# A decode block on one core: the wait ahead of the unit loop, and a full-width last chunk in the MLP

## The chip, the cores and the metric

One core of a Trainium2 chip runs the kernel. The metric is device time in microseconds (us) of one execution. Engines: TensorE (PE, with its weight loads as PEld), VectorE (DVE), ScalarE (ACT), GpSimd (POOL) and SyncE (SP), which issues nearly all DMA transfers from one in-order queue.

## The reference

Four tokens, each with its own cache of 4096 positions and 32 heads of 128. The caches are bf16 and fill nearly all of the 283 MB that are read.

```python
B, Sq, D, H, Sk, Dh, F = 4, 1, 640, 32, 4096, 128, 1728
q = (layernorm(x) @ wq)                      # per head, B x H x 1 x Dh
p = softmax(einsum("bhqd,bhkd->bhqk", q, k_cache) * Dh ** -0.5)
o = einsum("bhqk,bhkd->bhqd", p, v_cache)
h = x + o @ wo
f = layernorm(h) @ w1 + b1
sp = log1p(exp(-abs(f))) + where(f > 0, f, 0)
h2 = h + (f * tanh(sp)) @ w2                 # B x 1 x D, bf16
```

## The kernel before

**Units and slots.** The attention is cut into 16 units (`NU`), one token and eight heads each. A unit reads one K tile and one V tile of 128 partitions x 64 KiB (8.39 MB each). Three slots of that size in SBUF (`NS`) take them in turn: K of unit u goes into slot 2u mod 3 (unit 0: slot 1), and V of the same unit later into the same slot, once K is used up. Each slot has one DMA semaphore, `slot0` to `slot2`, that both loads count up. "K2" and "V2" stand for the loads of unit 2 below.

**A unit's work.** `scores` multiplies K by the broadcast query in eight steps on DVE (`times_q`, L585, in place), sums over the head dimension on PE through an identity (`sums`, L597), and reduces what is left on DVE (L572). `softmax` finds the maxima and takes the exponentials on ACT (L682). `pv` multiplies the probabilities of the unit before by its V (L707). `close` normalises the unit two before.

**Order.** The outer loop over u emits, for each unit: `scores(u)` (with pieces of `close(u-2)` and the query of u+1 in between), the load of V(u), `pv(u-1)`, the load of K(u+2), `softmax(u)`. So SP issues V(u) when PE has finished the sums of unit u, whose K lies in that slot, and K(u+2) when `pv(u-1)` is done with its slot.

**The planner.** A class `Program` collects the operations with what they read and write, and sets the semaphore waits. An operation has a key whose last entry is the unit in which it is emitted; a DMA has a semaphore of its own name in `sem`. All engines but PE run straight code. PE's work of units 2 to 13 is a hardware loop of 4 turns over 3 units (`Fori`, L200), whose waits count with the turn. Ahead of the loop PE waits for everything in `pe_entry` (L127 to 136, L198): for each source the latest operation that some PE step of the loop needs and that has no key or a key below unit 2. V1 is such an operation: it is loaded in unit 1 and read in unit 2 by `pv(1)`. `pv`'s own wait on the slot's semaphore is in the loop's body as well (`body_waits`).

**The end.** When K15 and V14 are used, their slots take the weights of the rest: SP issues four loads of wo, five of w1 (`load`, L823), the last 64 rows of w2 (`w2r_sb`), and w2's 13 full blocks of 128 rows in four loads. `load` waits for the last readers of the bytes that it overwrites; for w2 that is `last_pv`, which is `pv(14)`. Then `regroup` and `project` multiply by wo, `column_means` and three DVE steps make the second layernorm, `h1_pass` (L956) does the 14 column chunks of w1 for each of five row blocks, DVE and ACT make the activation `act_t` (a reciprocal and an exponential), and `w2_products` (L1024) sums the 14 chunks, the odd one first. F = 1728 is 13 x 128 + 64: `C2` = 13 full chunks, `FM` = 1664, `FREM` = 64, `FC` = 14 chunks in all. `f_chunk` gives the columns of a chunk; the last has 64, so the upper half of its partitions is set to zero in PSUM by DVE (L950) and in b1T by POOL (L389).

Of the kernel before, what the change touches and what calls it, by code (L numbers as in the profile page):

```python
# [21 lines left out]
class Program:  # L22
# [53 lines left out]
    def plan(self):  # L76
        by_key = {o.key: o for o in self.ops if o.key is not None}

        def shifted(o, units):
            return by_key.get((*o.key[:-1], o.key[-1] + units)) if o.key else None  # L80


        known = {e: {} for e in self.ENGINES}
        for o in self.ops:
            k = known[o.eng]
            o.waits = []
            for src, d in o.deps.items():
                if k.get(src, -1) < d.nth:
                    k[src] = d.nth
                    o.waits.append(d)  # L90


        span = self.last - self.first + 1
        assert span % self.turn == 0
        turns = span // self.turn
        self.turns = turns
        ref0 = self.first + 2 * self.turn
        body = [o for o in self.ops if self.in_loop(o) and ref0 <= o.key[-1] < ref0 + self.turn]
        self.body = body
        before, rest = [], None  # L100
        in_order = [o for o in self.ops if o.eng == "PE"]
        at = [i for i, o in enumerate(in_order) if self.in_loop(o)]
        assert at == list(range(at[0], at[0] + len(body) * turns))
        for t in range(turns):
            for p, b in enumerate(body):
                o = in_order[at[0] + t * len(body) + p]
                assert o is shifted(b, (t - 2) * self.turn), (o.key, b.key)
        self.pe_before = in_order[: at[0]]
        self.pe_after = in_order[at[0] + len(body) * turns :]
        body_waits = [[d for d in b.waits] for b in body]  # L110
        for b in body:
            for d in b.waits:
                assert d.key is not None and d.key[-1] >= self.first + self.turn, (b.key, d.key)


        loop_units = range(self.first, self.last + 1)
        for o in self.ops:
            for d in o.waits:
                d.signal = True
        for o in self.ops:  # L120
            if o.signal and o.key and o.key[-1] in loop_units:
                for u in range(self.first, self.last + 1):
                    same = by_key.get((*o.key[:-1], u))
                    if same is not None and same.sem is None:
                        same.signal = True

        self.pe_entry = {}  # L127
        first_pe = in_order[at[0]].nth
        for p in range(at[0], at[0] + len(body) * turns):
            for src, d in in_order[p].deps.items():  # L130
                if d.key is None or d.key[-1] < self.first:
                    e = self.pe_entry.get(src)
                    if e is None or e.nth < d.nth:
                        self.pe_entry[src] = d
        for d in self.pe_entry.values():
            d.signal = True

        counts = {}
        for o in self.ops:
            src = o.sem or o.eng  # L140
            if o.sem:
                counts[src] = counts.get(src, 0) + 16
            elif o.signal:
                counts[src] = counts.get(src, 0) + 1
            o.count = counts.get(src, 0)
        self.totals = counts


        self.body_waits = []
        for b, waits in zip(body, body_waits):  # L150
            out = []
            for d in waits:
                src = d.sem or d.eng
                e = shifted(d, self.turn)
                step = e.count - d.count
                assert step > 0
                for t in range(turns):
                    f = shifted(d, (t - 2) * self.turn)
                    if f is not None and f.key[-1] >= self.first:
                        assert f.count == d.count + (t - 2) * step, (b.key, d.key, t)  # L160
                base = d.count - 2 * step
                assert base > 0, (b.key, d.key)
                out.append((src, base, step))
            self.body_waits.append(out)


        level = {s: d.count for s, d in self.pe_entry.items()}
        for t in range(turns):
            for p, b in enumerate(body):
                for src, base, step in self.body_waits[p]:  # L170
                    level[src] = max(level.get(src, 0), base + t * step)
                o = in_order[at[0] + t * len(body) + p]
                for src, d in o.deps.items():
                    assert level.get(src, 0) >= d.count, (o.key, d.key, t)
# [35 lines left out]
def kernel(  # L210
# [13 lines left out]
    nc = tc.nc  # L224

    B, Sq, D = A_x.shape
    _, H, Sk, Dh = A_k_cache.shape
    F = B_w1.shape[1]
# [25 lines left out]
    FREM = F - FM  # L254
    FC = C2 + 1
    W2P = (0, 6, 10, 12, C2)


    pad = -int(nc.sbuf_base) % 512
# [126 lines left out]
        w=["ident_f"],  # L386
    )
    P.add("POOL", lambda: nc.gpsimd.memset(ones_f[:, :], 1.0), w=["ones_f"])
    P.add("POOL", lambda: nc.gpsimd.memset(b1T[:, :], 0.0), w=["b1T"])  # L389
    P.add("POOL", lambda: nc.gpsimd.memset(mean_f[:, :], 1.0 / D), w=["mean_f"])  # L390
    P.add("DVE", lambda: nc.vector.memset(eps_t[:, :], EPS), w=["eps"])
    P.add("DVE", lambda: nc.vector.memset(nscale[:, :], -SCALE), w=["nscale"])
# [93 lines left out]
        "DVE", lambda: nc.vector.tensor_copy(out=j_m[:, :], in_=j_f[:, :]), r=["j_f"], w=["j_m"]  # L486
    )

    def f_chunk(rows, c):
        if c < C2:  # L490
            return rows[:, c * 128 : (c + 1) * 128], 128
        return rows[:, FM:F], FREM


    qT_ps = qq_bank[:, 0 : N * H].rearrange("p (b h) -> p b h", b=N)

# [15 lines left out]

    def b1_turned():
        for c in range(FC):
            cols, fw = f_chunk(b1_row, c)
            ins = nc.tensor.matmul(  # L516
                b_ps[0:fw, c : c + 1], lhsT=cols, rhs=ident[0:1, 0:1], start=True, stop=True
            )
        return ins

    def b1_copy():
        nc.vector.tensor_copy(out=b1T[:, 0:C2], in_=b_ps[:, 0:C2])  # L522
        return nc.vector.tensor_copy(out=b1T[0:FREM, C2:FC], in_=b_ps[0:FREM, C2:FC])

    P.add("PE", b1_turned, r=["b1", "ident"], w=[OT])
    P.add("DVE", b1_copy, r=[OT], w=["b1T"])

    def q_broadcast(u, now):
        o, b = divmod(u, N)
# [279 lines left out]
    w1_view = B_w1.rearrange("(c p) n -> p c n", p=128)  # L809
    nw2 = FC * D  # L810
    w2_sb = wend2[:, 0 : C2 * D].rearrange("p (k n) -> p k n", k=C2)
    w2r_sb = wend2[0:FREM, C2 * D : nw2]
    w2_view = B_w2[0:FM, :].rearrange("(k p) n -> p k n", k=C2)

    def load(out_ap, in_ap, i, lo, hi, name):

        ops = {}
        for cell in cells(i, lo, hi):
            for d in P.readers.get(cell, {}).values():
                ops[d.nth] = d  # L820
        P.add(
            "SP",
            lambda: nc.sync.dma_start(out=out_ap, in_=in_ap),  # L823
            w=[name],
            sem="_".join(map(str, name)),
            after=ops.values(),
        )
# [2 lines left out]
        load(wo_sb[:, o], wo_view[:, o], i1, o * J * D, (o + 1) * J * D, ("wo", o))  # L830
    for c in range(DC):
        load(w1_sb[:, c], w1_view[:, c], i1, nwo + c * F, nwo + (c + 1) * F, ("w1", c))
    load(w2r_sb, B_w2[FM:F, :], i2, C2 * D, nw2, ("w2", C2))
    for k0, k1 in zip(W2P, W2P[1:]):
        load(w2_sb[:, k0:k1], w2_view[:, k0:k1], i2, k0 * D, k1 * D, ("w2", k0))

# [110 lines left out]
    tt(sq, hc, hc, ALU.mult, ["hc"], ["sq"])  # L947

    h1_ps = qq_bank[:, 0 : FC * N].rearrange("p (c n) -> p c n", c=FC)
    do("DVE", lambda: nc.vector.memset(h1_ps[FREM:128, FC - 1, :], 0.0), (), [QQ])  # L950
    std, rstd = scratch(N), scratch(N)

    def h1_pass(dc):
        for c in (0, C2, *range(1, C2)):
            lhsT, fw = f_chunk(w1_sb[:, dc, :], c)
            ins = nc.tensor.matmul(  # L956
                h1_ps[0:fw, c, :],
                lhsT=lhsT,
                rhs=h2T[:, dc, :],
                start=(dc == 0 and c == 0),  # L960
                stop=(dc == DC - 1 and c == C2 - 1),
            )
        return ins

# [53 lines left out]

    def w2_products(blocks):
        for c in blocks:  # L1020
            rows = 128 if c < C2 else FREM
            w2 = w2_sb[:, c, :] if c < C2 else w2r_sb
            for dc in range(DC):
                ins = nc.tensor.matmul(  # L1024
                    y2T[:, dc, :],
                    lhsT=w2[:, dc * 128 : (dc + 1) * 128],
                    rhs=act_t[0:rows, c, :],
                    start=(c == C2 and dc == 0),
                    stop=(c == C2 - 1 and dc == DC - 1),
                )  # L1030
        return ins

    for name, blocks in ((C2, [C2]), *((k0, range(k0, k1)) for k0, k1 in zip(W2P, W2P[1:]))):
        do("PE", lambda blocks=blocks: w2_products(blocks), [("w2", name), "act"], [S_BANK[1]])
    oT = scratch(N * DC, BF16).rearrange("p (n c) -> p n c", n=N)
    tt(oT.rearrange("p n c -> p c n"), hT, y2T, ALU.add, ["hT", S_BANK[1]], ["oT"])
    o_ps = tr_bank[0 : N * DC, 0:128]
# [45 lines left out]
```

## Time and profile before

| | |
|---|---|
| median of 3 runs | 672.83 us (672.2 to 672.95) |
| profiled execution | 673.69 us; its span, first to last instruction, 671.8 us; mean granted TensorE clock 0.818 |
| busy | PE 380.5 us (57%), DVE 353.2 (53%), ACT 88.0 (13%), POOL 1.3 |
| SP's DMA queue | 283.35 MB, busy 98.2% of 16 engines' span, mean 422 GB/s |
| chain that ended last | DMA 39%, DVE 28%, PE 20%, another queue or core 8%, SP's queue 3% |

Lines of the profile name the source line (L597), the engine, the operation, the tile written and the tiles read. A row of a timeline or a chain starts with its start and its length in us. In a table by stage each engine's busy time stands in the order PE, PEld, DVE, ACT, POOL, with the number of instructions in brackets, and then PE's granted clock, the DMA engines' busy share and GB/s. The releaser of a wait is inferred from semaphore events.

### The profile page before, as it was taken

To read this page: it belongs to the slowest core of one execution; us is meant where nothing else is said; L and a number is where in the kernel's file an instruction comes from. 1 tells how busy PE (TensorE), PEld (TensorE's weight loads), DVE (VectorE), ACT (ScalarE), POOL (GpSimd) and SP (SyncE) were. 2 spreads that over 40 slices of the span, in tenths; PEclk is the share of its full clock that TensorE was granted. 3 is DMA by queue.
4 is the path that set the end of the run, shared out by engine and by line. 5 is a ranking of instruction groups with operands and counts; after the bars stand their busy time and mean duration, and the time that the engine had idled before them with its cause. 6 is when DMAs were issued, how large, how long until landed. Compare 5 with 4: busy or idle time off the path is not lost.

```text
span 671.8 us, 6600 instructions
## 1 busy us (share of the span) xinstructions
PE 380.5 (57%) x2793; PEld 174.8 (26%) x2793; DVE 353.2 (53%) x314; ACT 88.0 (13%) x314; POOL 1.3 (0%) x10
## 2 busy tenths in 40 slices
PE   0366732887282856738184664818375481837764
PEld 0222310333031322213032321303132230313344
DVE  2078840766381836548182754728184563819501
ACT  0102020020202020110202020020202002020211
POOL 0000000000000000000000000000000000000000
PEclk9999975989596796959688796968879695978965
DMA  9999999799999999999999999999999999999997
GB/s 375 438 437 434 433 435 433 328 376 438 433 434 437 437 437 437 433 437 433 421 425 419 437 437 437 433 437 433 433 437 433 437 437 437 434 430 410 412 416 245
DMA packets 8347, 283.62 MB, mean 422 GB/s; under 512 B 835, under 2 KB 2567, under 8 KB 3208
## 3 DMA queue, kind: packets, MB, share of 16 engines
q1 hardware_dynamic: 8318, 283.35, 98.2%
q8 instruction: 12, 0.20, 0.1%
q14 instruction: 7, 0.06, 0.0%
q10 hardware_dynamic: 10, 0.01, 0.0%
HBM read 283.35 MB, written 0.01 MB: 422 GB/s over the span
## 4 chain that ended last, share of the span: by engine, by line
DMA 39%; DVE 28%; PE 20%; another core or an unknown queue 8%; SPq 3%; issue 1%
DMA slot<-in_A_k_cache_dram 33%; DVE slot L585 23%; PE bank L597 14%; PE bank L707 5%; DMA slot<-in_A_v_cache_dram 4%; DVE s_sb L572 3%; SPq L823 3%; DMA slot<-in_B_w_dram 2%; PE bank L665 0%; DVE mx L652 0%; PE bank L643 0%; DVE otn L767 0%; DVE rl L760 0%; PE bank L741 0%
## 5 line engine op out<-in xcount | busy, mean ns | idle before, releaser
L597 PE MATMUL bank<-slot,ident 128*128 128x512 bf16 x1024 | 273.9, 423 | 250.2 <-DVE slot L585 225.6
L585 DVE TENSOR_TENSOR slot<-slot,qb 128x4096 bf16<-128x4096 bf16 x128 | 288.2, 2284 | 145.4 <-DMA slot<-in_A_k_cache_dram 145.4
L597 PEld LDWEIGHTS bank<-slot,ident 128*128 128x128 bf16 x1024 | 101.5, 107 | 408.4 <-DVE slot L585 258.7
L572 DVE TENSOR_REDUCE s_sb<-bank 128x64 f32<-128x512 f32 x64 | 44.0, 688 | 74.5 <-PE bank L597 74.5
L682 ACT ACTIVATE e<-s_sb,nb 128x256 bf16<-128x256 f32 x128 | 63.1, 494 | 46.6 <-DVE nb L674 46.6
L707 PE MATMUL bank<-slot,e 128*32 128x512 bf16 x1024 | 60.7, 391 | 1.5 <-DMA slot<-in_A_v_cache_dram 1.5
L552 ACT CAST qb<-bank 128x128 bf16<-128x128 f32 x16 | 4.2, 265 | 294.5 <-PE bank L543 294.5
L727 ACT COPY o_sb<-bank 128x512 f32<-128x512 f32 x16 | 9.4, 585 | 200.2 <-PE bank L707 200.2
L707 PEld LDWEIGHTS bank<-slot,e 128*32 128x32 bf16 x1024 | 26.5, 99 | 34.1 <-issue 9.0
L652 DVE TENSOR_REDUCE mx<-bank 1x8 f32<-1x128 f32 x16 | 4.5, 279 | 39.9 <-PE bank L643 39.9
L682 ACT ACTIVATION_READ_ACCUMULATOR e<-s_sb,nb 128x1 f32 x128 | 23.9, 187 | 0.0
L741 PE MATMUL bank<-sel,o_sb 128*128 128x8 f32 x128 | 17.4, 263 | 0.0
L741 PEld LDWEIGHTS bank<-sel,o_sb 128*128 128x128 f32 x128 | 16.4, 201 | 0.0
L500 PE MATMUL bank<-xT,slot 128*128 128x4 bf16 x160 | 4.4, 168 | 11.0 <-DMA slot<-in_A_wq_dram 11.0
L665 PE MATMUL bank<-mx,nscale 1*128 1x8 f32 x32 | 6.1, 262 | 5.9 <-DVE mx L652 5.9
L760 DVE RECIPROCAL rl<-bank 128x8 f32<-128x8 f32 x16 | 3.2, 202 | 11.3 <-PE bank L741 11.3
L522 DVE COPY b1T<-bank 128x13 f32<-128x13 f32 x1 | 0.2, 172 | 14.5 <-PE bank L516 14.5
L665 PEld LDWEIGHTS bank<-mx,nscale 1*128 1x128 f32 x32 | 4.7, 183 | 10.6 <-DVE mx L652 10.6
L500 PEld LDWEIGHTS bank<-xT,slot 128*128 128x128 bf16 x160 | 4.3, 104 | 11.1 <-DMA slot<-in_A_wq_dram 11.1
L634 DVE TENSOR_REDUCE pm<-s_sb 128x1 f32<-128x256 f32 x16 | 6.7, 420 | 0.5
L739 PEld LDWEIGHTS bank<-rs,ones_f 128*128 128x128 f32 x32 | 6.1, 198 | 3.2 <-ACT o_sb L727 1.2
L643 PE MATMUL bank<-ident_f,pm 128*1 128x128 f32 x32 | 6.1, 272 | 1.2 <-DVE pm L634 1.2
(73 smaller groups left out, 69.2 us busy)
## 6 DMA issues: line engine op xcount, KB each, us to landing
slot<-in_A_v_cache_dram SPq DMA_DIRECT2D x4, 2048.0 KB, 42.5
slot<-in_A_wq_dram SPq DMA_DIRECT2D x1, 5120.0 KB, 15.5
slot<-in_A_wo_dram SPq DMA_DIRECT2D x4, 1280.0 KB, 33.8
slot<-in_B_w_dram SPq DMA_DIRECT2D x5, 432.0 KB, 29.7
slot<-in_B_w_dram SPq DMA_DIRECT2D x1, 960.0 KB, 20.4
slot<-in_B_w_dram SPq DMA_DIRECT2D x1, 640.0 KB, 19.5
slot<-in_B_w_dram SPq DMA_DIRECT2D x1, 320.0 KB, 10.9
slot<-in_A_k_cache_dram SPq DMA_DIRECT2D x16, 50.2
```

The source lines that it names most:

```text
L500: ins = nc.tensor.matmul(qT_ps[:, :, h], lhsT=wq_sb[:, c, h * Dh : (h + 1) * Dh], rhs=xT[:, c, :], start=(c == 0), stop=(c == DC - 1),)
L572: lambda: nc.vector.tensor_reduce(out=s_sb[:, part * RP : (part + 1) * RP], in_=s_bank[part][:, :].rearrange("p (r w) -> p r w", w=W), axi ...
L585: return nc.vector.tensor_tensor(out=kt, in0=kt, in1=qbs[u % NS][:, k * DQ : (k + 1) * DQ] .unsqueeze(1) .to_broadcast([128, RP, DQ]), op= ...
L597: ins = nc.tensor.matmul(s_bank[part][:, :].rearrange("p (r w) -> p r w", w=W), lhsT=ident[:, :], rhs=kt[:, :, d : d + W], start=(d == 0), ...
L634: lambda: nc.vector.tensor_reduce(out=pm[:, :], in_=s_sb[:, :], axis=AX.X, op=ALU.max),
L643: lambda: nc.tensor.matmul(tr_bank[0:1, 0:128], lhsT=pm[:, :], rhs=ident_f[:, :], start=True, stop=True),
L665: lambda: nc.tensor.matmul(nb_ps, lhsT=nscale[:, :], rhs=mx[:, :], start=True, stop=True),
L682: ins = nc.scalar.activation(out=e2[:, :, h, :], in_=s_sb[:, :].rearrange("p (g r) -> p g r", r=RQ), func=ACT.Exp, bias=nb[:, h : h + 1], ...
L707: ins = nc.tensor.matmul(o_bank[t : t + G * RQ, :], lhsT=e2[:, g, :, :], rhs=vt[:, g * RQ : (g + 1) * RQ, :], start=(g < CT), stop=(g >= N ...
L727: lambda: nc.scalar.copy(out=o_sb[:, :], in_=o_bank[:, :]),
L741: ins = nc.tensor.matmul(o_ps, lhsT=o_sb[:, r * Dh : (r + 1) * Dh], rhs=sel[:, r, :], start=(r == 0), stop=(r == RQ - 1),)
L823: lambda: nc.sync.dma_start(out=out_ap, in_=in_ap),
```

## The change

1. `pe_entry` takes only operations that are not transfers: an operation with a `sem` is left out. PE no longer waits for transfers ahead of the loop; the waits in the loop's body stay.
2. The last chunk of h1 covers the last 128 columns of w1 and b1 (1600 to 1727), so 64 columns are computed twice. `f_chunk`, POOL's memset of b1T and DVE's memset in PSUM go, the two copies of b1T become one, and the chunks are done in plain order.
3. w2's last 64 rows go to partitions 64 to 127 of `w2r_sb`; partitions 0 to 63 hold zeros, written over the whole tile by a new POOL memset that waits for `last_pv`. The load follows that memset, and PE's product of this chunk uses all 128 rows.

```diff
@@ -128,7 +128,8 @@
         first_pe = in_order[at[0]].nth
         for p in range(at[0], at[0] + len(body) * turns):
             for src, d in in_order[p].deps.items():
-                if d.key is None or d.key[-1] < self.first:
+
+                if d.sem is None and (d.key is None or d.key[-1] < self.first):
                     e = self.pe_entry.get(src)
                     if e is None or e.nth < d.nth:
                         self.pe_entry[src] = d
@@ -254,6 +255,7 @@
     FREM = F - FM
     FC = C2 + 1
     W2P = (0, 6, 10, 12, C2)
+    OVER = 128 - FREM
 
 
     pad = -int(nc.sbuf_base) % 512
@@ -386,7 +388,6 @@
         w=["ident_f"],
     )
     P.add("POOL", lambda: nc.gpsimd.memset(ones_f[:, :], 1.0), w=["ones_f"])
-    P.add("POOL", lambda: nc.gpsimd.memset(b1T[:, :], 0.0), w=["b1T"])
     P.add("POOL", lambda: nc.gpsimd.memset(mean_f[:, :], 1.0 / D), w=["mean_f"])
     P.add("DVE", lambda: nc.vector.memset(eps_t[:, :], EPS), w=["eps"])
     P.add("DVE", lambda: nc.vector.memset(nscale[:, :], -SCALE), w=["nscale"])
@@ -486,11 +487,6 @@
         "DVE", lambda: nc.vector.tensor_copy(out=j_m[:, :], in_=j_f[:, :]), r=["j_f"], w=["j_m"]
     )
 
-    def f_chunk(rows, c):
-        if c < C2:
-            return rows[:, c * 128 : (c + 1) * 128], 128
-        return rows[:, FM:F], FREM
-
 
     qT_ps = qq_bank[:, 0 : N * H].rearrange("p (b h) -> p b h", b=N)
 
@@ -512,18 +508,18 @@
 
     def b1_turned():
         for c in range(FC):
-            cols, fw = f_chunk(b1_row, c)
+            f0 = c * 128 if c < C2 else F - 128
             ins = nc.tensor.matmul(
-                b_ps[0:fw, c : c + 1], lhsT=cols, rhs=ident[0:1, 0:1], start=True, stop=True
+                b_ps[:, c : c + 1],
+                lhsT=b1_row[:, f0 : f0 + 128],
+                rhs=ident[0:1, 0:1],
+                start=True,
+                stop=True,
             )
         return ins
 
-    def b1_copy():
-        nc.vector.tensor_copy(out=b1T[:, 0:C2], in_=b_ps[:, 0:C2])
-        return nc.vector.tensor_copy(out=b1T[0:FREM, C2:FC], in_=b_ps[0:FREM, C2:FC])
-
     P.add("PE", b1_turned, r=["b1", "ident"], w=[OT])
-    P.add("DVE", b1_copy, r=[OT], w=["b1T"])
+    P.add("DVE", lambda: nc.vector.tensor_copy(out=b1T[:, :], in_=b_ps), r=[OT], w=["b1T"])
 
     def q_broadcast(u, now):
         o, b = divmod(u, N)
@@ -809,7 +805,7 @@
     w1_view = B_w1.rearrange("(c p) n -> p c n", p=128)
     nw2 = FC * D
     w2_sb = wend2[:, 0 : C2 * D].rearrange("p (k n) -> p k n", k=C2)
-    w2r_sb = wend2[0:FREM, C2 * D : nw2]
+    w2r_sb = wend2[:, C2 * D : nw2]
     w2_view = B_w2[0:FM, :].rearrange("(k p) n -> p k n", k=C2)
 
     def load(out_ap, in_ap, i, lo, hi, name):
@@ -830,7 +826,18 @@
         load(wo_sb[:, o], wo_view[:, o], i1, o * J * D, (o + 1) * J * D, ("wo", o))
     for c in range(DC):
         load(w1_sb[:, c], w1_view[:, c], i1, nwo + c * F, nwo + (c + 1) * F, ("w1", c))
-    load(w2r_sb, B_w2[FM:F, :], i2, C2 * D, nw2, ("w2", C2))
+    P.add(
+        "POOL",
+        lambda: nc.gpsimd.memset(w2r_sb, 0.0),
+        w=["w2r"],
+        after=[last_pv],
+    )
+    P.add(
+        "SP",
+        lambda: nc.sync.dma_start(out=w2r_sb[OVER:128, :], in_=B_w2[FM:F, :]),
+        w=["w2r"],
+        sem="w2r",
+    )
     for k0, k1 in zip(W2P, W2P[1:]):
         load(w2_sb[:, k0:k1], w2_view[:, k0:k1], i2, k0 * D, k1 * D, ("w2", k0))
 
@@ -947,18 +954,17 @@
     tt(sq, hc, hc, ALU.mult, ["hc"], ["sq"])
 
     h1_ps = qq_bank[:, 0 : FC * N].rearrange("p (c n) -> p c n", c=FC)
-    do("DVE", lambda: nc.vector.memset(h1_ps[FREM:128, FC - 1, :], 0.0), (), [QQ])
     std, rstd = scratch(N), scratch(N)
 
     def h1_pass(dc):
-        for c in (0, C2, *range(1, C2)):
-            lhsT, fw = f_chunk(w1_sb[:, dc, :], c)
+        for c in range(FC):
+            f0 = c * 128 if c < C2 else F - 128
             ins = nc.tensor.matmul(
-                h1_ps[0:fw, c, :],
-                lhsT=lhsT,
+                h1_ps[:, c, :],
+                lhsT=w1_sb[:, dc, f0 : f0 + 128],
                 rhs=h2T[:, dc, :],
                 start=(dc == 0 and c == 0),
-                stop=(dc == DC - 1 and c == C2 - 1),
+                stop=(dc == DC - 1 and c == C2),
             )
         return ins
 
@@ -1018,20 +1024,20 @@
 
     def w2_products(blocks):
         for c in blocks:
-            rows = 128 if c < C2 else FREM
             w2 = w2_sb[:, c, :] if c < C2 else w2r_sb
             for dc in range(DC):
                 ins = nc.tensor.matmul(
                     y2T[:, dc, :],
                     lhsT=w2[:, dc * 128 : (dc + 1) * 128],
-                    rhs=act_t[0:rows, c, :],
+                    rhs=act_t[:, c, :],
                     start=(c == C2 and dc == 0),
                     stop=(c == C2 - 1 and dc == DC - 1),
                 )
         return ins
 
-    for name, blocks in ((C2, [C2]), *((k0, range(k0, k1)) for k0, k1 in zip(W2P, W2P[1:]))):
-        do("PE", lambda blocks=blocks: w2_products(blocks), [("w2", name), "act"], [S_BANK[1]])
+    do("PE", lambda: w2_products([C2]), ["w2r", "act"], [S_BANK[1]])
+    for k0, k1 in zip(W2P, W2P[1:]):
+        do("PE", lambda b=range(k0, k1): w2_products(b), [("w2", k0), "act"], [S_BANK[1]])
     oT = scratch(N * DC, BF16).rearrange("p (n c) -> p n c", n=N)
     tt(oT.rearrange("p n c -> p c n"), hT, y2T, ALU.add, ["hT", S_BANK[1]], ["oT"])
     o_ps = tr_bank[0 : N * DC, 0:128]
```

## The prediction

> **What bounds the kernel now.** I read the page first, its slices and its DMA queues: the queue that SyncE (SP) feeds is busy 98.2% of the span, and the row of GB/s stands near 435 except at the start, at the end, and in the eighth and ninth slices (118 to 151 us).
>
> ```profile
> GB/s 375 438 437 434 433 435 433 328 376 438 433 434 437 437 437 437 433 437 433 421 425 419 437 437 437 433 437 433 433 437 433 437 437 437 434 430 410 412 416 245
> ...
> q1 hardware_dynamic: 8318, 283.35, 98.2%
> ```
>
> So this is a stream of transfers, and what matters is when it stands still. The busy time by stage around the dip (stretch, length, the engines' busy time, granted clock, DMA share, GB/s) shows that it does so once:
>
> ```profile
> 117.50:130.30 12.80, 11.34 (x52) 5.17 (x50) 9.89 (x8) 0.27 (x1) 0.00 (x0) 0.92 1.01 435
> 130.30:136.00 5.70, 4.25 (x28) 1.71 (x32) 3.71 (x4) 0.00 (x0) 0.00 (x0) 1.00 0.01 3
> 136.00:140.00 4.00, 3.63 (x64) 1.79 (x56) 0.97 (x3) 0.58 (x1) 0.00 (x0) 1.00 1.16 426
> ```
>
> For 5.7 us nothing moves. SP's own rows say why: between two issues of cache loads lie 47 us, which is more than two transfers last.
>
> ```profile
> 88.60 0.33 SPq L333 DMA_DIRECT2D slot<-in_A_k_cache_dram  x1
> 135.62 0.33 SPq L333 DMA_DIRECT2D slot<-in_A_v_cache_dram  x1
> 139.21 0.33 SPq L333 DMA_DIRECT2D slot<-in_A_k_cache_dram  x1
> ```
>
> The load at 135.62 is V of unit 2 (V2 below). It goes into the slot of K2, so it waits until PE has summed all of K2 (`sums`, L597). What held PE is in the waits from 86 to 140 us (sum, times, longest) and in the chain that ended last (start, length, what):
>
> ```profile
> PE bank L597 <- DMA slot<-in_A_v_cache_dram: 24.6, 1, 24.6
> ```
>
> ```profile
> 85.03 28.73 DMA slot<-in_A_v_cache_dram
> 113.75 0.33 issue
> 114.08 6.27 PE bank L597 x16
> ```
>
> K2 had landed at 94.42, where VectorE (DVE) began its products (L585). PE stood until V1 landed at 113.75, although nothing reads V1 before `pv` of unit 1, which PE does after all sums of unit 2. This is the wait ahead of the loop (L198): `pe_entry` holds V1, whose key is unit 1 and so below the loop's first unit, 2.
>
> **The entry wait.** With the new condition transfers drop out of `pe_entry`. What is left there is the engines' work of earlier units, the last of it ScalarE's exponentials of unit 1 (last accumulator row 93.56 + 0.19 = 93.75), and PE's own wait inside the loop for the first product of K2 (94.42 + 2.30 = 96.72). So PE starts at about 96.8 and not at 114.08. Unit 4 shows an undisturbed unit: its products start at 178.02 and its `pv` at 201.13, 23.1 us later. Unit 2 then ends its sums at 94.42 + 23.1 = 117.5; V2 is issued there, 18 us earlier than now. V1 has landed by then (113.75), so the wait that moves to `pv` costs nothing, with a margin of 3.8 us; `pv` takes 3.6, and K4 is issued near 121.2.
>
> K3 is still moving until 130.3, so V2 stands in the queue 12.8 us before the engines run dry, and the stretch of 5.7 us closes. I size the gain by landings, because these hold the restart too. From 216.98 (K5) to 449.29 (K11) lie 12 transfers: 232.31 / 12 = 19.36 us each. From K2 (94.42) to K4 (178.02) are 4 transfers: 83.60, where 4 x 19.36 = 77.44. The difference is 6.16 us. The low end is the standstill alone, 5.7; the high end adds that K4 to K5 took 38.96 and not 38.72, 0.24 more, so 6.4. I take 6.16, as it is measured at a landing.
>
> Does the stall come back later? K3 lands near 94.42 + 2 x 19.36 = 133.1, and V3 can be issued 23.1 us later, at 156.2; the queue then holds K4 until about 169.1 (landing at 171.9, less 2.8 between a stream's last bytes and the landing, as 130.3 is to 133.1). That is some 13 us in hand. From there on each unit needs about 27 us of engine time (23.1 + 3.6) while its two transfers need 38.7, and the later rows show DVE waiting 10 to 11 us for each K. The rest of the stream therefore moves forward as one block, and K15, now at 604.38, lands near 598.2.
>
> **The last chunk, start of the kernel.** Removed: one GpSimd (POOL) memset of b1T, 0.11 us at 2.10, in front of a memset whose reader comes at 657; and one of two DVE copies (0.14 us at 21.62), after which DVE idles 14.4 us for K0. V0's issue at 21.57 waits for PE, not for the copy. Nothing on the path: 0. If DVE's idle time were gone it would be 0.14 gained.
>
> **The zeros and the moved load.** Before, the load of w2's 64 odd rows waits for `last_pv` on PE (ends 631.21). Now a POOL memset of 128x640 waits for that, and SP waits for the memset. The four other w2 loads and the output stand behind it on SP. POOL's rows give 0.110 us for 14 columns and 0.204 for 128, so 0.110 + 626 x 0.094 / 114 = 0.63 us for 640; bounds 0.2 (flat) and 5 x 0.204 = 1.0. SP gets to this load late, since its issues by then go only as fast as the queue drains:
>
> ```profile
> 638.37 3.17 SPq L823
> 641.59 2.66 SPq L823
> 644.30 2.64 SPq L823
> 646.98 9.44 SPq L823
> 656.46 10.90 DMA slot<-in_B_w_dram
> 667.40 0.71 PE bank L1024 x15
> ```
>
> The sixth of the ten w1 and w2 issues, at 641.59, is the odd rows (80 KB, landing 20.5 us later). 641.59 - 631.21 = 10.4 us of cover for a memset of at most 1.0: cost 0. Without that cover it would cost 0.2 to 1.0. The same 80 KB to other partitions: 0, give or take the 0.2 us that 80 KB take at 433 GB/s.
>
> **h1 and w2 on PE.** The removed memset of PSUM (L950, 0.06 us) is what PE waits for at 658.92; without it PE starts after the first h2T subtraction, near 658.4, so up to 0.5 us sooner. Against this, five h1 matmuls get 128 columns in place of 64: from nothing to double, 5 x 0.047 (70 matmuls in 1.31 + 1.97 us) = 0.23. Five w2 matmuls get 128 rows, count unchanged: 0 to 0.2. The new order of the chunks changes no count. None of it sets the end: `act` is ready at 664.58, the first w2 matmuls start at 664.72 when 960 KB have landed (issued 644.30, 20.4 to landing), and PE then waits again for 0.63 and 0.20 us for the last loads. The end is the landing at 667.36 plus 4.4 us. I take 0; ends -0.5 to +0.2.
>
> **Sum.** The profiled execution took 673.69 (span 671.8 and 1.89 around it), 0.86 over the median of 672.83. 673.69 - 6.16 = 667.5 for a like execution; against the median, 672.83 - 6.16 = 666.7. A measurement here tells about 0.2% (1.35 us) from no change.
>
> **Rivals.** (1) *The wait only changes its name.* PE's release at 114.08 is inferred, and if another wait of the loop ends there, nothing moves: 672.8. Against it: the products, the exponentials and the previous reductions were done by 96.72, and the only row that ends near 114 is V1's. 3 in 100.
>
> (2) *The transfers are slower when nothing stops them, and swallow the gap.* The stall exists only because K3 is through before V2 is issued; with transfers of over 135.62 - 113.75 = 21.9 us there would be none, and its removal would be worth 0: 672.8. The rows show 19.36 us from unit 5 to unit 11 without any standstill: 1 in 100. The Trainium skill (DMA: Bandwidth & Descriptors, "Where 436 GB/s comes from") says that for loads from HBM a limit of about 358 GB/s per core binds, not the 435 of the ports; by it a transfer would take some 23.4 us (an estimate) and the change would bring nothing. The trace disagrees: 433 to 437 GB/s, the ports' figure.
>
> (3) *Part of it is given back*, by a new wait of V3 or K4 on PE or in SP's order: with half lost, 669.8. The margins above (3.8 and 13 us) speak against it. 4 in 100.
>
> (4) *Slower: the memset holds SP.* Place: the load at 641.59, with four w2 loads behind it. It decides once the memset ends over 10.4 us after `last_pv`; after that SP's delay first eats the queue, which holds about 19 us (landing 20.5 us after issue, little of it its own). To end over 0.2% slower the memset must last 10.4 + 19 + 6.2 + 1.4 = 37 us; at 40 us the time would be 666.7 + 40 - 29.4 = 677. For it: no POOL row of this size exists, and no POOL row runs beside DVE late in the kernel. Against: 0.63 from POOL's rows, and DVE is busy only 3.07 us of 628 to 636. 3 in 100, with other mishaps of that sign. The Trainium skill (SBUF — State Buffer, "Who interferes with whom") says that GpSimd and a DVE instruction in a two-port mode shut each other out for a whole instruction. By the longest DVE row near there, 0.68 us, that makes 1.3 us and leaves the sum alone; no run here shows it yet.
>
> **Numbers.** The forecast holds 89 in 100. Its own range: gain 5.7 to 6.4, tail -0.5 to +0.2, and 0.4 either way for the spread of the runs (672.2 to 672.95) give 665.5 to 667.7. The upper end goes a little further into case 3: 665.6 to 668.0. Faster 0.93 (forecast and case 3), same 0.04 (cases 1 and 2), slower 0.03.
>
> **What would show it.** PE's first sums of unit 2 near 96.8; V2 issued near 117.5 and K4 near 121; no standstill at 130 to 136; K4 landing at 171.9 and K15 at 598.2; the POOL memset under 1.3 us and over before SP gets to the odd rows; from the last w2 landing to the end 4.4 us as now. It is wrong if SP waits for POOL, if another stretch without transfers appears, or if the first product of unit 4 starts later than 173.

## The result and the profile after

The changed kernel takes 668.38 us in the median (668.24 to 668.61, 6 runs) where the kernel before takes 672.90 (672.20 to 673.37, 6 runs): ratio 0.9934, 95% interval 0.9921 to 0.9946. The gain is 4.5 us. Forecast were 6.2 and 666.7, with 668.0 as the upper end of the range: the direction is right, the size is not.

The standstill is gone. In the same stretches as before (same columns) the DMA share is 1.04 where it was 0.01, and PE has little left to do there:

```profile
117.50:130.30 12.80, 3.87 (x68) 1.86 (x56) 1.30 (x4) 4.81 (x18) 0.00 (x0) 0.75 1.00 432
130.30:136.00 5.70, 0.48 (x2) 0.21 (x3) 2.83 (x2) 0.00 (x0) 0.00 (x0) 0.50 1.04 448
136.00:140.00 4.00, 4.00 (x11) 1.43 (x10) 3.86 (x2) 0.00 (x0) 0.00 (x0) 0.50 0.95 410
```

PE's timeline shows it start on unit 2 at 96.80, released by DVE's first product and no longer by V1, and end its sums at 117.2. SP's timeline has V2 and K4 behind that, at 117.28 and 120.87:

```profile
96.80 6.93 PE L593 MATMUL bank<-slot,ident 128*128 128x512 bf16 x24 [7.37 <-DVE slot L581]
...
117.14 3.64 PE L703 MATMUL bank<-slot,e 128*32 128x512 bf16 x64
```

```profile
88.56 0.33 SPq L335 DMA_DIRECT2D slot<-in_A_k_cache_dram  x1
117.28 0.33 SPq L335 DMA_DIRECT2D slot<-in_A_v_cache_dram  x1
120.87 0.33 SPq L335 DMA_DIRECT2D slot<-in_A_k_cache_dram  x1
```

DVE's timeline, whose idle time ends with each K's landing, had K4 at 178.02 and K15 at 604.38 before:

```profile
178.02 6.70 DVE L585 TENSOR_TENSOR slot<-slot,qb 128x4096 bf16<-128x4096 bf16 x3 [10.23 <-DMA slot<-in_A_k_cache_dram]
...
604.38 6.70 DVE L585 TENSOR_TENSOR slot<-slot,qb 128x4096 bf16<-128x4096 bf16 x3 [10.26 <-DMA slot<-in_A_k_cache_dram]
```

Now it has K3 at 133.16, K4 at 171.90 and K15 at 598.08:

```profile
133.16 6.70 DVE L581 TENSOR_TENSOR slot<-slot,qb 128x4096 bf16<-128x4096 bf16 x3 [11.22 <-DMA slot<-in_A_k_cache_dram]
...
171.90 6.70 DVE L581 TENSOR_TENSOR slot<-slot,qb 128x4096 bf16<-128x4096 bf16 x3 [10.13 <-DMA slot<-in_A_k_cache_dram]
...
598.08 6.70 DVE L581 TENSOR_TENSOR slot<-slot,qb 128x4096 bf16<-128x4096 bf16 x3 [9.88 <-DMA slot<-in_A_k_cache_dram]
```

So at K15 the kernel is 604.38 - 598.08 = 6.3 us ahead, as forecast. But its span is only 671.8 - 666.5 = 5.3 shorter. One microsecond is given back after K15. PE's rows of the last stage show where: V15's last quarter, then the third and the fourth block of wo. Before:

```profile
643.52 1.04 PE L707 MATMUL bank<-slot,e 128*32 128x512 bf16 x16 [1.47 <-DMA slot<-in_A_v_cache_dram]
...
652.81 1.23 PE L892 MATMUL bank<-slot,slot 128*128 128x4 bf16 x40 [1.61 <-DMA slot<-in_A_wo_dram]
...
655.92 1.23 PE L892 MATMUL bank<-slot,slot 128*128 128x4 bf16 x40 [1.89 <-DMA slot<-in_A_wo_dram]
```

And now:

```profile
638.04 1.05 PE L703 MATMUL bank<-slot,e 128*32 128x512 bf16 x16 [1.89 <-DMA slot<-in_A_v_cache_dram]
...
647.33 1.23 PE L899 MATMUL bank<-slot,slot 128*128 128x4 bf16 x40 [1.63 <-DMA slot<-in_A_wo_dram]
...
650.75 1.23 PE L899 MATMUL bank<-slot,slot 128*128 128x4 bf16 x40 [2.19 <-DMA slot<-in_A_wo_dram]
```

Most of it, 0.8 us, is there by V15's last quarter, which now comes 39.96 us after K15 (39.14 before); the blocks of wo are 3.42 us apart in place of 3.11.

That leaves two gaps: 1.0 us between K15 and the end, and 0.9 us between the two profiles' 5.45 (673.69 - 668.24) and the medians' 4.5. The profiled execution of before, from which I took all durations, was 0.8 slower than the median of its kernel, and that of the changed kernel 0.14 faster.

### The profile page after: what moved, and what is told of

It is laid out like the page before. It is cut to its first block, busy times and chain, and to the rows that moved or that the text cites. A ratio compares the mean times of both kernels' runs of the same rounds, so it can differ in the third digit from the quotient of the medians.

```text
span 666.5 us, 6596 instructions
## 1 busy us (share of the span) xinstructions
PE 377.2 (57%) x2793; PEld 173.0 (26%) x2793; DVE 353.2 (53%) x312; ACT 87.9 (13%) x314; POOL 1.9 (0%) x10
## 4 chain that ended last, share of the span: by engine, by line
DMA 36%; DVE 28%; PE 21%; another core or an unknown queue 12%; SPq 2%; issue 1%
DMA slot<-in_A_k_cache_dram 27%; DVE slot L581 24%; PE bank L593 14%; DMA slot<-in_A_v_cache_dram 7%; PE bank L703 6%; DVE s_sb L568 4%; SPq L819 2%; DMA slot<-in_B_w_dram 2%; PE bank L661 0%; DVE mx L648 0%; PE bank L639 0%; DVE otn L763 0%; DVE rl L756 0%; SPq L335 0%
## 5 line engine op out<-in xcount | busy, mean ns | idle before, releaser
L899 PE MATMUL bank<-slot,slot 128*128 128x4 bf16 x160 | 4.7, 166 | 3.8 <-DMA slot<-in_A_wo_dram 3.8
```

## The experiments

**First set: is it the length of the standstill, or the last stage?** Theory A says that the standstill differs from execution to execution and was long in the first profile; B puts the rest on the new chunk and its loads; C on the missing standstill itself.

*e1_before_again* is the kernel before, with no edit.

> The kernel before, unchanged, for a second profiled execution. The first one took 673.69 us, 0.8 over the median of its runs. Theory A (the standstill of the DMA queue is not of one length: it ends when unit 2's sums are done, and the first 16 of them, at PE's half clock after 24.6 us of idling, took 6.27 us in the first profile where other units took 4.9 to 6.6): here the 16 take less, K4 lands earlier than 178.0 by that difference (near 177.2), the span is near 671.0, and from K15's first product to the end it is 67.4 us as before. Theory B (the standstill is always worth 6.2 and the difference lies in the last stage): K4 lands at 178.0 within 0.1 and the last stage is some 0.8 us shorter than 67.4. Time by both: ratio 1.000.

Measured: 673.16 (11 runs), ratio 0.9996 (0.9987 to 1.0005); span 671.4. The chain of waits has the first 16 sums at 5.60 us (6.27 in the first profile), and SP issues V2 at 135.14 (135.62):

```profile
114.27 5.60 PE bank L597 x16
```

K4 lands at 177.44, 0.58 earlier, and from K15 (603.95) to the end it is 67.45, as in the first profile (67.4). Theory A holds for the standstill; the 16 sums took 0.7 less and K4 landed 0.6 earlier, in place of the 0.8 expected, and the span fell by 0.4 (671.0 expected).

*e2_entry_only* keeps part 1 of the change alone.

```diff
-                if d.key is None or d.key[-1] < self.first:
+                if d.sem is None and (d.key is None or d.key[-1] < self.first):
```

> Only the first part of the change: no transfers in the entry wait; chunk, zeros and w2's rows as before. Theory A: K15's first product near 598.3 and 668.4 us, as the whole change. Theory B with the last stage lengthened by parts 2 and 3 (from K15 to the end 68.2 us in the changed kernel against 67.4 before): 667.6 to 667.8 here, and 67.4 from K15 to the end. Theory C (without the standstill the queue comes to the last stage differently, whatever the weights' loads are): 68.2 from K15 to the end here too, 668.4.

Measured: 668.51 (5 runs), ratio 0.9926 (0.9913 to 0.9940): the whole gain. K15 at 598.19, span 666.8, so 68.6 from K15 to the end, and 3.63 between the two wo blocks: the last stage is longer without any of the new loads.

*e3_chunk_only* keeps parts 2 and 3 alone: the changed kernel with the old condition in `pe_entry`.

```diff
-                if d.sem is None and (d.key is None or d.key[-1] < self.first):
+                if d.key is None or d.key[-1] < self.first:
```

> Only parts 2 and 3 of the change: full-width last chunk, zeros by POOL, w2's odd rows on the last partitions; the entry wait as before. Theories A and C: 672.9, nothing within 0.3. Theory B: 673.6, 0.7 slower, all of it after K15.

Measured: 673.20 (11 runs), ratio 0.9997 (0.9988 to 1.0006). The full-width chunk, the zeros and the moved load cost and bring nothing. K15 at 603.11, span 670.6: 67.5 from there. With e2 this rules out B.

*e4_warm_pe* and *e5_warm_to_end* keep the entry wait, but fill PE's wait for V1 with extra matmuls, 185 and then 214.

```diff
+    WARM = 185
...
+    def warm():
+        for _ in range(WARM):
+            ins = nc.tensor.matmul(
+                tr_bank[:, 256:512].rearrange("p (a b) -> p a b", a=2),
+                lhsT=ident[:, :],
+                rhs=ident[:, :].unsqueeze(1).to_broadcast([128, 2, 128]),
+                start=True,
+                stop=True,
+            )
+        return ins
...
+        if u == 2:
+            P.add("PE", warm, r=["ident"], w=[TR])
```

> The kernel before with the entry wait, but PE does 185 extra matmuls of the identity into unused columns of a bank (results not used) while it waits for V1, so that its clock is at full rate when unit 2's sums begin. Theory A: the first 16 sums take 3.5 to 3.9 us in place of 6.3, V2 is issued 2.4 to 2.8 us earlier (near 133), the standstill falls from 5.7 to near 3.1, K4 lands near 175.4, and the time falls by 2.0 to 2.8 (670.1 to 670.9). If the clock has nothing to do with the standstill's length: 672.9.

Measured: 672.95 (11 runs), ratio 0.9998 (0.9989 to 1.0007): a miss. The extra work ended at 110.3, PE idled 3.8 us until V1 landed, and the clock granted from 114 to 119 was 0.66; the first 16 sums took 5.24.

> As e4_warm_pe, whose extra matmuls ended at 110.3, 3.8 us before V1 landed, so that the clock fell again (0.66 from 114 to 119 us): now 214 of them, ending near 113.6 (results not used). If the standstill's length is set by the first 16 sums (theory A): these take 3.5 to 3.8 us, V2 is issued near 133.0, K4 lands 42.45 us after that (the mean of four runs with the standstill, 42.30 to 42.59), near 175.4, K15's first product follows 426.3 later at 601.7, the end 67.4 after that: span 669.1, time near 670.9. If not: 672.9 to 673.4.

Measured: 671.04 (670.83 to 671.32, 8 runs), ratio 0.9970 (0.9960 to 0.9981). The clock stays at 1.00 and the sums take 3.64, by the chain of waits; SP issues V2 at 133.21:

```profile
114.31 3.64 PE bank L598 x16
```

```profile
133.21 0.33 SPq L334 DMA_DIRECT2D slot<-in_A_v_cache_dram  x1
```

So the clock with which PE comes out of its wait sets the length of the standstill. In five profiles (before, e1, e3, e4, e5) the time from PE's start to V2's issue, less the first 16 sums, is 15.26 to 15.27 us, while the sums themselves run from 3.64 to 6.27. The runs close up as well: 0.5 us apart here, 2.1 apart in the 21 runs of before beside them (672.22 to 674.29, median 673.11). The Trainium skill (TensorE: Matmul & The Clock Gate, "Part 1: The HAM clock gate") says that the clock halves after an idle window of about 3.4 us, that it takes as long to come back, and that the window runs freely, so that the number of slow matmuls differs between runs of one kernel. The traces agree: the granted clock is 0.50 from 114 to 117 us in the first profile, after 24.6 us of idling, 0.66 from 114 to 119 in e4 after 3.8, and 1.00 in e5 after 1.2; and with the entry wait the same 16 matmuls take 5.17 to 6.27 us where PE has idled.

**Second set: why the last stage is longer without a standstill.** Theory D (C made definite): the 16 DMA engines fall out of step, and a standstill lets the late ones catch up. Theory E: something else about a kernel without the entry wait. *e6_reset_mid* puts a standstill back by other means; *e7_reset_late* does so for V14 and K15 (`("K", 0, 15)` and `u == 14` in the lines below). Both have part 1 of the change, and `load_kv` passes `after` on.

```diff
...
-            load_kv("V", v_rows, u, slot_of(u))
+            held = [x for x in P.ops if x.key == ("K", 0, 3)] if u == 2 else ()
+            load_kv("V", v_rows, u, slot_of(u), after=held)
```

> The entry-only kernel, with one added wait: SP issues V2 only when K3 has landed (133.4). PE stands as it does there, so the queue runs dry in the same place as before, from another cause and for a shorter time, some 3 us. V2 issued near 133.4, K4 near 175.9, K15's first product near 602.2. Theory D (the 16 DMA engines fall out of step by the delays that single ones take, and only a standstill lets the late ones catch up): from there to the end 67.3 to 67.5 as in the four profiles with a standstill; span near 669.6, time 671.4. Theory E (the last stage is longer for some other reason in kernels without the entry wait): 68.4 to 68.6 as in the two profiles without one; 672.4.

Measured: 671.50 (8 runs), ratio 0.9975 (0.9965 to 0.9986). V2 issued at 133.55, K4 at 176.07, K15 at 602.25, span 669.9: 67.65 from K15 to the end, and the wo blocks are 3.10 apart again, by PE's timeline:

```profile
650.96 1.23 PE L894 MATMUL bank<-slot,slot 128*128 128x4 bf16 x40 [1.70 <-DMA slot<-in_A_wo_dram]
...
654.06 1.22 PE L894 MATMUL bank<-slot,slot 128*128 128x4 bf16 x40 [1.87 <-DMA slot<-in_A_wo_dram]
```

> The entry-only kernel, with one added wait: SP issues V14 only when K15 has landed (598.2), some 3 us after the queue has run dry there. V15's last quarter then lands 42.8 us after V14's issue, near 641.1. Theory D: the engines are in step again for the last stage, wo's third and fourth block are worked on 3.1 us apart as in the four profiles with a standstill, and from V15's last part to the end it is 28.2 to 28.3; span 669.4, time 671.2. Theory E: 3.4 to 3.6 us between these two blocks and 28.5 to 28.8 to the end as in the two without; time 671.5 or more.

Measured: 671.28 (10 runs), ratio 0.9973 (0.9963 to 0.9982), span 669.2. V15's last part at 640.92 (641.1 expected), wo blocks 3.10 apart, 28.3 to the end. Both side with D: the last stage is short when the queue has run dry once, wherever and why ever that was. e6 shows it by its 67.65 (0.15 over D's range, 0.75 under E's). e7's two measures alone would not: of the kernels below without a standstill, e9 also has 28.3 from V15's last part to the end, and e11 3.12 between the blocks. What tells them apart is in the traces, which hold 16 landing signals of each of these transfers, as many as there are DMA engines (K3's in the first profile come 0.4 to 0.5 us after the ends of its last 16 rows, one by one). For wo's fourth block the last of the 16 comes 1.1 to 1.3 us after their mean in the seven profiles with a standstill, e7 (1.13) among them, and 1.7 to 2.1 after it in the six without one (the changed kernel, e2, and e8 to e11).

*e8_after_again* is the changed kernel once more.

> The changed kernel again, for a second profiled execution. From K15's first product (598.1 to 598.3) to the end 68.3 to 68.7 if the longer last stage belongs to the kernel, 67.4 if it was chance in two executions. Time 668.4, ratio 0.993.

Measured: 668.75 (4 runs), ratio 0.9938 (0.9922 to 0.9955). K15 at 598.28, span 666.8: 68.5, wo blocks 3.50 apart. The longer last stage belongs to the kernel. The profiles side by side, with e9 of the third set (e7, e10 and e11 are left out, as their last stage has a standstill or loads of its own):

| kernel | V2 issued | K15's first product | span | V2's issue to end | K15 to end | wo blocks apart |
|---|---|---|---|---|---|---|
| before | 135.62 | 604.38 | 671.8 | 536.2 | 67.4 | 3.11 |
| e1_before_again | 135.14 | 603.95 | 671.4 | 536.3 | 67.5 | 3.12 |
| e4_warm_pe | 134.60 | 603.51 | 670.8 | 536.2 | 67.3 | 3.12 |
| e3_chunk_only | 134.44 | 603.11 | 670.6 | 536.2 | 67.5 | 3.11 |
| e6_reset_mid | 133.55 | 602.25 | 669.9 | 536.4 | 67.7 | 3.10 |
| e5_warm_to_end | 133.21 | 601.95 | 669.2 | 536.0 | 67.3 | 3.11 |
| after | 117.28 | 598.08 | 666.5 | | 68.4 | 3.42 |
| e2_entry_only | 117.25 | 598.19 | 666.8 | | 68.6 | 3.63 |
| e8_after_again | 118.71 | 598.28 | 666.8 | | 68.5 | 3.50 |
| e9_memset_25us | 117.59 | 597.97 | 666.3 | | 68.3 | 3.29 |

The fifth column is the sum that I should have made. With a standstill the kernel ends 536.2 us (536.0 to 536.4) after V2's issue. Without one it ends where a V2 issued at 666.5 - 536.2 = 130.3 to 130.6 would put it (130.1 by e9). That is about where the last of K3's rows starts (130.2 in the packets of the first trace). So in these profiles the gain is V2's issue less 130.3 to 130.6, to within some 0.3 us. The sum fits the profiles; it does not say why.

**Third set: what the moved load could have cost, and a better version.** *e9_memset_25us* and *e10_memset_40us* lengthen POOL's work ahead of w2's odd rows (2 x 15000 and 3 x 16000 columns).

```diff
+    for _ in range(2):
+        P.add(
+            "POOL",
+            lambda: nc.gpsimd.memset(wend2[:, 16384 : 16384 + 15000], 0.0),
+            w=["fill"],
+            after=[last_pv],
+        )
```

> The changed kernel, with two more POOL memsets of 15000 columns into unused columns of the same slot ahead of the one of w2's rows (they change nothing in the result): by POOL's rows 0.1 + 15000 x 0.000825 = 12.4 us each, so that SP is held at w2's odd rows until about 650.9, 14.8 us after it gets there (636.1). As the prediction prices it, SP's delay first eats the queue of 18 to 19 us (w1's last rows move until about 654.5): no change, 668.4 to 668.8. If SP's order counts at once: 683.

Measured: 668.51 (4 runs), ratio 0.9931 (0.9915 to 0.9946). POOL's and SP's timelines show SP held until 651.36, 15.2 us later than in the changed kernel, at no cost: the queue still holds work (415 GB/s from 636 to 651 us, 414 in the changed kernel), and the later loads then go out in 0.6 us each.

```profile
625.50 25.25 POOL L832 MEMSET slot<- 128x15000 bf16 x2 [623.20 <-PE bank L703]
650.70 0.63 POOL L838 MEMSET slot<- 128x640 bf16 x1
```

```profile
651.36 0.56 SPq L844 DMA_DIRECT2D slot<-in_B_w_dram  x1
651.97 2.53 SPq L819 DMA_DIRECT2D slot<-in_B_w_dram  x4
```

> The same with three memsets of 16000 columns, some 40 us: SP held until about 665.8, 29.7 us late. As the prediction prices it 29.7 - 19 = 10.7 us slower, 679.2; by landings, the queue is empty at about 654.5, and w2 (6.5 us) and its landing (2 us) follow 665.8: last landing near 675 where it was 662.07, 681.

Measured: 681.33 (4 runs), ratio 1.0117 (1.0101 to 1.0132). SP issues the odd rows at 666.21, 30.1 us late, PE waits 11.8 us for them, and the last load is used at 675.29 (662.07): the count by landings gave 681, the count by the queue's 19 us 679.2, which is 2.1 too little.

*e11_w2_long_rows* is the changed kernel with longer pieces of w2.

```diff
+    def f_cols(rows, c):
+        if c < C2:
+            return rows[:, 0:FM].rearrange("p (m k) -> p k m", k=C2)[:, c, :]
+        return rows[:, F - 128 : F]
...
-                lhsT=b1_row[:, f0 : f0 + 128],
+                lhsT=f_cols(b1_row, c),
...
-    w2_view = B_w2[0:FM, :].rearrange("(k p) n -> p k n", k=C2)
+    w2_view = B_w2[0:FM, :].rearrange("(p k) n -> p k n", k=C2)
...
-                lhsT=w1_sb[:, dc, f0 : f0 + 128],
+                lhsT=f_cols(w1_sb[:, dc, :], c),
```

> A version meant to beat both: the changed kernel, with w2's 13 full blocks cut so that a partition holds 13 neighbouring rows (row p*13 + k in place of k*128 + p), and w1's and b1's columns taken with a step of 13 to match. The last stage moves only 307 to 364 GB/s from 652 to 660, since w2 comes in pieces of 1280 bytes: 60 ns each, where 1280 bytes at the 27.1 GB/s of a long row are 47. 1664 pieces x 12.5 ns / 16 engines = 1.3 us. PE has 1.9 us of waiting in h1 to hide weights that are read with a step. Expected 0.8 to 1.3 us less than 668.5: 667.2 to 667.7. If the stage is bound by the activation chain and not by w2's landing: 668.5.

Measured: 667.82 (667.64 to 668.02, 5 runs), ratio 0.9919 (0.9906 to 0.9933): the fastest of all, 0.6 to 0.9 below the changed kernel and 0.7 below e9 beside it. That is a little less than expected (667.2 to 667.7): w2 is no longer what ends last. By PE's timeline all 70 products of w2 now run without a wait once the activation is there, and h1 takes longer, since each load of weights that are read with a step of 13 takes 161 ns at the median where it took 104:

```profile
655.49 2.56 PE L965 MATMUL bank<-slot,slot 128*128 128x4 bf16 x42
660.25 2.01 PE L1032 MATMUL bank<-slot 128*128 128x4 bf16 x70 [2.20 <-DVE slot L1007]
```

## Why the prediction was right and wrong

**Right, step by step.** The wait ahead of the loop was for V1, and it alone carries the gain (e2). PE's start (96.8 forecast, 96.80 measured), V2's issue (117.5, 117.28), K4's issue (121.2, 120.87), K4's landing (171.9, 171.90) and K15's (598.2, 598.08) came as worked out, and no stall came back. POOL's memset took the 0.63 us read off from two of POOL's rows, beside a DVE row of 0.28 us that took as long before; it was over at 625.88, 10.2 us before SP got to the load. Beside the 25 us of memsets in e9, too, DVE's rows are as long as before (0.68 and 0.23 us), so no run here shows the two engines shutting each other out. Parts 2 and 3 are on no path, as forecast (e3: ratio 0.9997). The end follows the last w2 landing by 4.4 us, as before.

Of the rivals, the entry wait did not change its name, and the stream did not slow down: K4 to K15 is 426.2 us now and 426.4 before. The 358 GB/s that the Trainium skill gives at the place cited there do not bind here: the table by stage has 432 to 448 GB/s from 117.5 to 136 us. Rival 3, that part of the gain is given back, came true by 1.0 us, but not by the waits that it named: V3 and K4 were issued in time, and the loss lies behind K15. Of the slower rival, e9 and e10 bear out the kind of price: 15 us late cost nothing, 30 us late cost 12.8, some 2 us more than its sum gives.

**Wrong: the size, in two terms.** First, "I size the gain by landings, because these hold the restart too ... I take 6.16", with the tail behind K15 put at 0 (-0.5 to +0.2). The landings did come 6.1 us (K4) and 6.3 us (K15) earlier, but the end only 5.3: the step that fails is that what a landing shows reaches the end unchanged. A landing is the last of 16 signals. Their mean in the two profiles, and how far the last lies behind it, show what happened:

| landing of | mean before | mean after | difference | last behind mean, before | after | difference of the last |
|---|---|---|---|---|---|---|
| K4 | 176.68 | 170.86 | 5.8 | 1.32 | 1.01 | 6.1 |
| K15 | 602.95 | 597.12 | 5.8 | 1.41 | 0.94 | 6.3 |
| wo, fourth block | 654.70 | 648.88 | 5.8 | 1.17 | 1.83 | 5.2 |
| w2, the load that PE waits for last | 666.31 | 660.36 | 5.9 | 1.05 | 1.66 | 5.3 |

The mean is 5.8 to 5.9 us ahead from K4 to the end. The K landings show more, because there the last signal is later behind its mean in the kernel before, and the end shows less, because there it is later in the changed kernel. That is the 1.0 us between K15 and the end.

Counted at V2's issue the profiled execution loses 135.62 - 130.45 = 5.2; but 130.45 is the middle of the 130.3 to 130.6 that come from the measured spans, so this restates the result. The low end of the forecast, 5.7, was nearer than the landing that I chose, but it rests on a misread row. The table by stage counts a packet in the stretch in which it starts (so a share can be over 1: 1.16 in the row behind the standstill), and rows that start before 130.30 are still moving after it. By the packets of that trace the last 16 rows of K3 end between 130.7 and 132.6, and V2's first 16 start between 136.6 and 137.4: no cache row moves for 4.0 us, and an engine is idle for 5.4 on the mean. The 2.8 us from a stream's last bytes to its landing have the same fault: K3's last row ends at 132.61, its last signal comes at 133.10.

Second, the last line of the sum, "against the median, 672.83 - 6.16". It takes the standstill of one execution for that of the kernel. That execution was 0.8 over the median, and the standstill is what differs: its first 16 sums took 6.27 where three other profiles with the same wait have 5.17 to 5.60. Between the two profiled executions 5.45 of the 6.16 are left (5.3 of span and some 0.1 around it). Of these, 0.79 is how far the first one lies above its median (673.69 against 672.90), and 0.14 how far the second lies below its own (668.24 against 668.38): 5.45 - 0.79 - 0.14 = 4.52, the measured gain. By the three later sets, where the median of before is 673.41 (27 runs), 673.11 (21) and 673.44 (9), the first of these would be 0.3 to 0.6. The stated range failed because its low gain, 5.7, was a figure of that one execution too.

**Shown and inferred.** Shown: with a standstill, of whatever cause, the last stage is 0.7 to 1.3 us shorter (six profiles against four, two of the six with the entry wait's standstill replaced or shortened), and the landing signals of the last loads lie closer together. Inferred: how the engines come to be out of step. The trace holds start, length and size of each packet but not its engine. Joined into 16 chains, each packet following one that ends as it starts, the 64 KiB rows take 2.42 us each, and rows beside a packet of the two instruction queues mostly 0.4 to 0.7 longer. The chains' last 64 KiB rows end 2.9 us apart in the changed kernel, the last one 0.95 after the next; before, 2.2 apart and 0.1. That fits delays which hit single engines and pile up until the queue runs dry. Chains in step can be confused with one another, so which engine took which delay stays open, and taking the instruction fetches away wasn't tried.

## What to carry to other kernels

In a kernel that lives on one stream of transfers, do not size a standstill by two landings alone: a landing shows the latest engine, and how late that one is differs from place to place and with the standstill itself. Here the last signals were 6.1 to 6.3 us ahead at the K landings and 5.3 at the end, with means 5.8 to 5.9 ahead throughout. Look also at where a table of stretches puts a packet that lasts over a border. Before subtracting a stall from a median, ask whether it is the part that varies: the profiles of e1, e4 and e3, with the same wait, have spans 0.4 to 1.2 us shorter than the one that I reckoned with. And where a wait looks dangerous on an in-order queue, its price is the delay less the work that is already queued behind it in the DMA engines: here 15 us cost nothing and 30 cost 12.8.

## What the runs showed of the hardware

- A standstill leaves its mark after it ends: the first sixteen 64 KiB rows then take 2.7 to 3.4 us in the first profile (2.42 otherwise), and 2.4 to 3.5 over all seven standstills, 3.0 to 3.1 on the mean. In the changed kernel's stream no such group of slow rows appears.
- The last of a transfer's 16 landing signals can come 1 to 2 us after their mean: on wo's fourth block 1.1 to 1.3 in the seven profiles whose queue ran dry once, 1.7 to 2.1 in the six whose queue did not.
- One engine's 64 KiB row is mostly 0.4 to 0.7 us longer beside a 16 KiB or 8 KiB packet of the instruction queues (2.80 to 3.08 us in the changed kernel's trace, 2.42 otherwise). There are 12 and 7 of these on the page's list of queues of the kernel before, too few to show in any rate.
- PE's clock after a wait set the time of a kernel that is bound by transfers: 2.6 us less for the first 16 sums (e5 against the first profile) gave 2.6 us less span (669.2 against 671.8), and 2.1 us less time by the medians (671.04 against 673.11).
- POOL's memset stays close to linear far beyond the rows that I had: 0.63 us for 640 columns of bf16, 12.6 for 15000, 13.5 for 16000.
